# Blocks of 448 query tokens in place of 512 in an attention and two-expert-layer kernel

## The chip, the cores and the metric

The kernel runs on one core of a Trainium2 chip. The metric is the device time of one execution in microseconds (us). PE is the tensor engine, DVE the vector engine, ACT the scalar engine, POOL the GpSimd engine, and SP the engine that issues most transfers. Per-instruction durations are in nanoseconds (ns).

## The reference

The inputs are `q`, `k`, `v` of 12480 tokens by 128 values, 49 agents of 128 values, and four weight matrices between 128 and 2048 values in double precision. The reference computes

```python
scale = 1.0 / np.sqrt(128)
a2k = softmax(scale * agents @ k.T)      # 49 x 12480
agent_v = a2k @ v                        # 49 x 128
q2a = softmax(scale * q @ agents.T)      # 12480 x 49
x = q2a @ agent_v                        # 12480 x 128
h = np.maximum(x @ w_in, 0)
x = (s * h * h + b) @ w_out              # first expert layer
h = np.maximum(x @ w_in2, 0)
out = (h * h) @ w_out2                   # second expert layer
```

## The kernel before

**Precision.** Each large operand is split into two 32-bit words with short mantissas, `hi` and `lo`, whose sum is the operand (`split`, lines 115 to 118). A product then takes two matrix multiplications (`up1`, where the softmaxed scores `X` hold both words in the rows of one operand) or three (`up2` and both `down` products): `lo*hi`, `hi*lo` and `hi*hi`, accumulated in one PSUM bank.

**Stages.** Before the expert layers the kernel goes over keys and values in groups of 1024 tokens (`kblocks`, not part of the change), decodes the double precision weights on DVE between other work (`w_decode`, `fill`), and makes `M`, the agents' values times `w_in` (`m_piece`). So the first layer's up product goes straight from the agent softmax `X` to the hidden values.

**Blocks and steps.** The 12480 queries are cut into blocks by `cut`. A block is `(first token, partitions p, tokens of each partition j)` and holds `n = p * j` tokens; `n` is also the number of columns that every matrix multiplication of its expert layers streams. `cut(4)` gives 24 blocks of 512 (128 partitions of four) and a rest of 192. Because the rest is under 256, the code shares it out with the block before: the list ends with 23 blocks of 512, one of 384 and one of 320, 25 in all. The hidden width of 2048 is 16 chunks of 128, and a step handles two chunks, so that a block has 8 steps (`NPR`). The loop of lines 590 to 634 runs over steps of all blocks in one sequence, and in each step issues, in this order:

- `up1` (line 534): 4 matrix multiplications of the current step, and small pieces of the next block's agent softmax: transposes of its queries (line 133), scores (line 169 with the transposes of line 184, or line 159 for the first four blocks), the exponential, and the stacking transposes of line 215;
- `up2` (line 545): 6 matrix multiplications of the step that is 11 earlier (`L2`);
- `down` of the first layer (line 556): 6 of the step 2 earlier (`LAG`);
- `down` of the second layer (line 556 too): 6 of the step 13 earlier;
- once in 8 steps `store` (line 583): 4 transposes of a finished block's output, a copy, and its transfer.

That is 22 matrix multiplications in a full step, 176 for a block, each with its own weight load. After each `up`, `hidden` runs Relu (line 521) and Square (line 522) on ACT over both chunks at once (1024 elements a partition for a block of 512), then the two parts of `split` on DVE (lines 117 and 118). In steps 1 to 9 the second part runs on POOL instead. Decoding of weights (lines 258 to 278) goes on in DVE's time until about step 19, by a list of operations a step (`FILL_L`).

The order on each engine is written by hand: the program order above is the order of each queue. `ps_h` has two buffers, `ps_y` one for each layer, `ps_m` two.

Of the kernel before, what the change touches and what calls it, by code (L numbers as in the profile page):

```python
# [14 lines left out]
AX = mybir.AxisListType  # L15

P = 128
LAST = 320  # tokens of the last block where the rest is short
LAG = 2  # steps between the two products of a layer
WC = 512  # columns of a weight matrix decoded at a time  # L20
RAW = 4  # weight pieces, groups of keys and groups of values on chip ahead of their use
KB = 5
VB = 7
FIRST = "kwkkwkwkw"  # order of the first loads: keys, weights
# Weight decoding on the vector engine: operations between the others, by phase.
FILL_K = (2, 4, 5, 5, 5, 5, 4, 4, 4, 4, 4, 4, 2, 0)
FILL_T = 1
FILL_V = (5,) * 5 + (3,) * 6 + (1, 0)
QS = (0, 1, 2, 3, 4, 6)  # steps of a block in which the next one's agent softmax is worked on
DIRECT = 4  # blocks before this one have their scores by token at once, with more work on the tensor engine  # L30
M_AT = (2, 3)  # steps before which the last columns of M are made
FM = (2, 2)
FILL_L = (2,) * 6 + (3,) * 5 + (2,) * 2 + (3,) * 10
W_MIN = 2.0**-15
# [4 lines left out]
def tile_agent_attention_two_moe(  # L39
# [15 lines left out]
    _, N, C = q.shape  # L55
# [5 lines left out]
    GAP = 64  # L61
    KS = GAP + NA

    def cut(rows):
        """Token pieces (first token, partitions, tokens of each partition)."""
        pieces, t = [], 0
        while N - t >= rows * P:
            pieces.append((t, P, rows))
            t += rows * P
        if t < N:  # L70
            left = N - t
            p = next(x for x in range(min(P, left), 0, -1) if left % x == 0 and left // x <= rows)
            pieces.append((t, p, left // p))
        return pieces

    blocks = cut(4)
    if len(blocks) > 1 and blocks[-1][1] * blocks[-1][2] < 256:
        # Products this short wait for their weights: the last two blocks share their tokens.
        left = N - blocks[-2][0]
        if left % 4 == 0 and (left - LAST) // 4 <= P:  # L80
            blocks[-2:] = [(blocks[-2][0], (left - LAST) // 4, 4), (N - LAST, LAST // 4, 4)]
    kblocks = cut(8)
    NT = sum(j for _, _, j in kblocks)

# [4 lines left out]
    q, k, v, agents = q[0], k[0], v[0], agents[0]  # L89
# [23 lines left out]
    Xs = [const.tile([KS, 2, 256], F32R, name=f"X{i}") for i in range(2)]  # L113

    def split(dst, src, eng_lo, copy=nc.vector.tensor_copy):
        """dst[0] + dst[1] == src, each with a short mantissa."""
        copy(dst[0], src)  # L117
        eng_lo.tensor_tensor(out=dst[1], in0=src, in1=dst[0].bitcast(F32), op=ALU.subtract)  # L118

# [1 line left out]
    q_raw, qT, q_sT, q_e, q_st, X = {}, {}, {}, {}, {}, {}  # L121

    def q_load(t):
# [26 lines left out]
        q_e[t] = e  # L150

    def q_scores(t):
        """Scores by token, less their maximum."""
        _, p, j = blocks[t]
        x = qT.pop(t)
        ps = ps_m.tile([P, 512], F32, tag="m", name="ps_s")
        sc = ps[:p, :j * NA].rearrange("p (j n) -> p j n", n=NA)
        for i in range(j):
            nc.tensor.matmul(out=sc[:, i], lhsT=x[:, i * p:(i + 1) * p], rhs=aT[:, :NA], start=True, stop=True)
        q_shift(t, sc)  # L160

    def q_scores_T(t):
        """Scores by agent: the agents' short mantissas above, the rest below. The block's halves then go above each other."""
        _, p, j = blocks[t]
        n = p * j
        x = qT.pop(t)
        ps = ps_m.tile([P, 512], F32, tag="m", name="ps_sT")
        for z in (1, 0):
            nc.tensor.matmul(out=ps[:KS, :n], lhsT=aS, rhs=x[z][:, :n], start=(z == 1), stop=(z == 0))  # L169
        sT = sTs[t % 2]  # L170
        for h, to in halves:
            nc.scalar.copy(sT[to, :2 * p], ps[:NA, 2 * p * h:2 * p * (h + 1)])
        for h, to in halves:
            nc.vector.tensor_tensor(
                out=sT[to, :2 * p], in0=ps[GAP:KS, 2 * p * h:2 * p * (h + 1)], in1=sT[to, :2 * p], op=ALU.add
            )
        q_sT[t] = sT
# [29 lines left out]
        q_st[t] = st  # L207

    def q_stack(t):
        """The block's halves come out above each other: each keeps its short mantissas there, the rest goes to the other's rows."""  # L210
        _, p, j = blocks[t]
        st = q_st.pop(t)
        ps = ps_m.tile([P, 512], F32, tag="m", name="ps_x")
        for i in range(2):
            nc.tensor.transpose(  # L215
                out=ps[:KS, i * p:(i + 1) * p],
                in_=st[:p, 2 * i:2 * i + 2].rearrange("p h n -> p (h n)")[:, :KS],
                identity=ident[:p, :p],
            )
        x = Xs[t % 2]  # L220
        places = (0, slice(0, NA), slice(GAP, KS)), (1, slice(GAP, KS), slice(0, NA))
        for h, own, _ in places:
            nc.scalar.copy(x[own, h, :2 * p], ps[own, :2 * p])
        for h, own, other in places:
            nc.vector.tensor_tensor(
                out=x[other, h, :2 * p], in0=ps[own, :2 * p], in1=x[own, h, :2 * p].bitcast(F32), op=ALU.subtract
            )
        X[t] = x[:, :, :2 * p]
# [2 lines left out]
    dec_p = ctx.enter_context(tc.tile_pool(name="dec_p", bufs=3))  # L231

    def w_load(src, i):
        """512 columns of a double precision matrix, as words."""
        t = raw_p.tile([P, WC, 2], I32, tag="raw", name="raw")
        words = src.bitcast(I32)
        if src.shape[0] == P:
            nc.sync.dma_start(
                out=t, in_=words[:, 2 * WC * i:2 * WC * (i + 1)].rearrange("p (f w) -> p f w", w=2)
            )  # L240
        else:
            m = WC // C
            nc.sync.dma_start(
                out=t.rearrange("p (m c) w -> p m (c w)", c=C),
                in_=words[m * P * i:m * P * (i + 1), :].rearrange("(m p) c -> p m c", p=P),
            )
        return t

    def w_decode(raw, hi, lo, early):
        """Double to hi (12 bits of significand) + lo (the 24 bits behind them, rounded)."""  # L250
        L, H = raw[:, :, 0], raw[:, :, 1]
        x = dec_p.tile([P, WC], I32, tag="x", name="x")
        li = dec_p.tile([P, WC], I32, tag="li", name="li")
# [27 lines left out]
    wo_f = [x.rearrange("p m c -> p (m c)") for x in wo]  # L281
    wo2_f = [x.rearrange("p m c -> p (m c)") for x in wo2]

    # Weights are decoded in the vector engine's spare time, two pieces by turns.
    to_load, loaded, running, done = [], [], [], []
    wi = wo2_f  # free until the second layer's last weights come
    for src, pair in ((w_in, wi), (w_out, wo_f), (w_in2, wi2), (w_out2, wo2_f)):
        for i in range(NW):
            to_load.append((src, i, pair))
# [4 lines left out]
            loaded.append((w_load(src, i), i, pair))  # L294

    def fill(n):
        """The next n operations of the decoding; a freed buffer is loaded again."""
        for _ in range(n):
            if len(running) < 2 and loaded and (not running or min(x[1] for x in running) >= 4):
                raw, i, pair = loaded.pop(0)  # L300
# [16 lines left out]
                next_load()  # L317

    def finish(n):
        """Until no more than n pieces are left to decode."""  # L320
        while len(to_load) + len(loaded) + len(running) > n:
            fill(1)

    def m_piece(i):
        """512 columns of the values of the agents times w_in, the same in both halves of the rows."""
        sl = slice(i * WC, (i + 1) * WC)
        ps = ps_m.tile([P, 512], F32, tag="m", name="ps_M")
        for z, (x, w) in enumerate(((av[0], wi[1]), (av[1], wi[0]), (av[0], wi[0]))):
            nc.tensor.matmul(out=ps[:KS], lhsT=x, rhs=w[:, sl], start=(z == 0), stop=(z == 2))
        split((M[0][:, sl], M[1][:, sl]), ps[:KS], nc.vector, nc.scalar.copy)  # L330

    with tc.manual_schedule():
# [1 line left out]
        with tc.tile_pool(name="pre", bufs=1) as pre, tc.tile_pool(name="kp", bufs=2) as kp:  # L334
            NG = len(kblocks)
            ag = pre.tile([NA, C], F32, name="ag")
# [36 lines left out]
                else:  # L373
                    next_load()

            # The tensor engine's clock rises while the first loads are under way.
            ps = ps_m.tile([P, 512], F32, tag="m", name="ps_w")
            for i in range(16):
                nc.tensor.transpose(out=ps[:, :P], in_=ident, identity=ident)
# [65 lines left out]
            ps_cs = ps_y.tile([P, 512], F32, tag="y2", name="ps_cs")  # L445

            def colsum(a, e):
                """Column sums of w_out on every partition: the constant in the first activation adds b times them."""
                for n in range(a, e):
                    w = wo_f[n % 2][:, n // 2 * WC:(n // 2 + 1) * WC]  # L450
                    nc.tensor.matmul(out=ps_cs, lhsT=ones_r, rhs=w, start=(n == 0), stop=(n == 2 * NW - 1))
# [58 lines left out]
                m_piece(i)  # L510
                fill(FM[i])

# [1 line left out]
        ep = ctx.enter_context(tc.tile_pool(name="ep", bufs=2))  # L514
        gp = ctx.enter_context(tc.tile_pool(name="gp", bufs=3))
        L2 = NPR + LAG + 1
# [11 lines left out]
        def up1(t, i):  # L528
            n = blocks[t][1] * blocks[t][2]
            ps = ps_h.tile([P, 2, 512], F32, tag="h", name="ps_h1")  # L530
            for c in range(2):
                sl = slice((2 * i + c) * P, (2 * i + c + 1) * P)
                for z in (1, 0):
                    nc.tensor.matmul(out=ps[:, c, :n], lhsT=M[z][:, sl], rhs=X[t], start=(z == 1), stop=(z == 0))  # L534
            # The vector engine still decodes weights while the first steps run.
            G1[t, i] = hidden(ps, n, 1, nc.gpsimd if 1 <= t * NPR + i < L2 - 1 else nc.vector)

        def up2(t, i):
# [51 lines left out]
        for st in range(total + L2 + LAG + 3):  # L590
            t, i = divmod(st, NPR)
# [73 lines left out]
```

## Time and profile before

| | us |
|---|---|
| three timed runs | 1154.88, 1157.58, 1157.71 |
| median of the runs | 1157.58 |
| profiled execution: span from the first to the last instruction | 1152.7 |
| median less that span | 4.9 |
| PE busy in the span | 1130.1 |
| DVE busy in the span | 961.9 |
| ACT busy in the span | 923.2 |

The profiled execution's own time is not recorded apart from its span; the 4.9 us between span and median are start and end of an execution. "Busy" is the union of an engine's instructions; matrix multiplications are pipelined and overlap, so that the mean duration of one is longer than the distance between two starts. That distance is called the pitch below.

### The profile page before, as it was taken

The numbers are of one execution on the slowest core, as the hardware profiler recorded it, in microseconds if no ns is written. First come the engines' busy times: TensorE is split into PE (matmuls) and PEld (weight loads), VectorE is DVE, ScalarE is ACT, GpSimd is POOL, SyncE is SP. The second block draws the span as 40 slices with busy tenths as digits, with TensorE's granted clock in tenths as the row PEclk, the third lists the DMA queues.
The fourth block names the chain that finished last, engine by engine and source line by source line (L and its number), as shares of the span: only waits on it lengthen the run. The fifth ranks groups of instructions, "written<-read, shape, count | busy, mean of one in ns | idle before, by whom it ended". The sixth has DMA issues, their size and how long they took to land.

```text
span 1152.7 us, 14084 instructions
## 1 busy us (share of the span) xinstructions
PE 1130.1 (98%) x5297; PEld 927.3 (80%) x5297; DVE 961.9 (83%) x1293; ACT 923.2 (80%) x1067; POOL 38.1 (3%) x45
## 2 busy tenths in 40 slices
PE   8997899999999999999999999999999999999998
PEld 8975688888888888888888888888888888888897
DVE  5889998888888888888888888888888888888875
ACT  4646788888888888888888888888888888888885
POOL 1315100000000000000000000000000000000000
PEclk9899999999999999999999999999999999999999
DMA  8860000000000000000000000000000000000000
GB/s 316 243 192 34 1 1 19 19 1 19 19 1 19 19 1 19 19 1 19 19 1 19 19 1 19 19 1 19 19 1 19 19 1 17 15 1 10 10 11 13
DMA packets 27356, 34.88 MB, mean 30 GB/s; under 512 B 1767, under 2 KB 18488, under 8 KB 27288
## 3 DMA queue, kind: packets, MB, share of 16 engines
q1 hardware_dynamic: 27000, 33.98, 9.2%
q8 instruction: 42, 0.69, 0.3%
q14 instruction: 26, 0.21, 0.1%
q10 hardware_dynamic: 288, 0.00, 0.0%
HBM read 27.58 MB, written 6.39 MB: 29 GB/s over the span
## 4 chain that ended last, share of the span: by engine, by line
PE 88%; DVE 5%; ACT 1%; issue 1%; POOL 0%; DVEq 0%; ACTq 0%
PE ps_y L556 46%; PE ps_h L545 24%; PE ps_h L534 15%; PE ps_o L583 1%; PE ps_sT L169 1%; PE ps_q L133 1%; DVE gh L117 1%; ACT r L521 1%; DVE x L264 0%; PE ps_x L215 0%; POOL gl L118 0%; DVE x L270 0%; ACT r L522 0%; DVE li L266 0%; PE ps_b L184 0%
## 5 line engine op out<-in xcount | busy, mean ns | idle before, releaser
L521 ACT ACTIVATE r<-ps_h 128x1024 f32<-128x1024 f32 (+2 forms) x400 | 400.1, 1000 | 145.8 <-PE ps_h L534 121.6
L118 DVE TENSOR_TENSOR gl<-r,gh 128x1024 fp32r<-128x1024 f32 (+2 forms) x391 | 468.5, 1198 | 13.4
L522 ACT ACTIVATE r<-r 128x1024 f32<-128x1024 f32 (+2 forms) x400 | 416.1, 1040 | 12.7
L117 DVE CAST gh<-r 128x1024 fp32r<-128x1024 f32 (+2 forms) x400 | 273.1, 683 | 144.0 <-ACT r L522 139.0
L545 PE MATMUL ps_h<-yh,wi2l 128*128 128x512 f32 (+2 forms) x400 | 162.0, 405 | 2.0 <-DVE yh L117 1.7
L556 PE MATMUL ps_y<-gl,woh 128*128 128x512 f32 (+2 forms) x400 | 156.7, 392 | 5.6 <-POOL gl L118 5.0
L534 PE MATMUL ps_h<-X,Ml 113*128 113x512 f32 (+2 forms) x400 | 158.5, 397 | 1.6 <-DVE Ml L118 0.8
L556 PE MATMUL ps_y<-gh,wol 128*128 128x512 f32 (+2 forms) x400 | 157.7, 394 | 0.5 <-ACT y L564 0.5
L556 PE MATMUL ps_y<-gl,wo2h 128*128 128x512 f32 (+2 forms) x400 | 157.1, 393 | 0.6 <-DVE gl L118 0.6
L534 PE MATMUL ps_h<-X,Mh 113*128 113x512 f32 (+2 forms) x400 | 156.7, 392 | 0.0
L556 PE MATMUL ps_y<-gh,wo2l 128*128 128x512 f32 (+2 forms) x400 | 156.6, 392 | 0.0
L545 PE MATMUL ps_h<-yl,wi2h 128*128 128x512 f32 (+2 forms) x400 | 156.4, 391 | 0.2 <-DVE yl L118 0.2
L545 PE MATMUL ps_h<-yh,wi2h 128*128 128x512 f32 (+2 forms) x400 | 156.5, 391 | 0.0
L556 PE MATMUL ps_y<-gh,wo2h 128*128 128x512 f32 (+2 forms) x400 | 156.2, 391 | 0.0
L556 PE MATMUL ps_y<-gh,woh 128*128 128x512 f32 (+2 forms) x400 | 156.0, 390 | 0.0
L556 PEld LDWEIGHTS ps_y<-gl,woh 128*128 128x128 f32 x400 | 75.4, 189 | 25.4 <-POOL gl L118 7.1
L534 PEld LDWEIGHTS ps_h<-X,Ml 113*128 113x128 f32 x400 | 75.9, 190 | 19.1 <-issue 1.2
L556 PEld LDWEIGHTS ps_y<-gh,woh 128*128 128x128 f32 x400 | 76.0, 190 | 17.3
L556 PEld LDWEIGHTS ps_y<-gh,wol 128*128 128x128 f32 x400 | 75.4, 188 | 17.8 <-ACT y L564 0.9
L534 PEld LDWEIGHTS ps_h<-X,Mh 113*128 113x128 f32 x400 | 75.9, 190 | 16.8
L556 PEld LDWEIGHTS ps_y<-gl,wo2h 128*128 128x128 f32 x400 | 75.2, 188 | 17.1 <-DVE gl L118 1.1
L556 PEld LDWEIGHTS ps_y<-gh,wo2h 128*128 128x128 f32 x400 | 75.2, 188 | 17.1
(122 smaller groups left out, 989.5 us busy)
## 6 DMA issues: line engine op xcount, KB each, us to landing
kraw<-in_k_dram SPq DMA_DIRECT2D x12, 512.0 KB, 7.6
v<-in_v_dram SPq DMA_DIRECT2D x12, 512.0 KB, 7.6
q_raw<-in_q_dram SPq DMA_DIRECT2D x23, 256.0 KB, 2.7
out_dram<-o SPq DMA_DIRECT2D x23, 256.0 KB, 2.0
raw<-in_moe_w_in_dram SPq DMA_DIRECT2D x8, 512.0 KB, 7.2
raw<-in_moe_w_out_dram SPq DMA_DIRECT2D x8, 512.0 KB, 5.1
q_raw<-in_q_dram SPq DMA_DIRECT2D x1, 192.0 KB, 2.6
out_dram<-o SPq DMA_DIRECT2D x1, 192.0 KB, 2.1
```

The source lines that it names most:

```text
L117: copy(dst[0], src)
L118: eng_lo.tensor_tensor(out=dst[1], in0=src, in1=dst[0].bitcast(F32), op=ALU.subtract)
L133: nc.tensor.transpose(out=ps[:, i * p:(i + 1) * p], in_=raw[:p, i], identity=ident[:p, :p])
L169: nc.tensor.matmul(out=ps[:KS, :n], lhsT=aS, rhs=x[z][:, :n], start=(z == 1), stop=(z == 0))
L521: nc.scalar.activation(r[:, :, :n], ps[:, :, :n], AF.Relu)
L522: nc.scalar.activation(r[:, :, :n], r[:, :, :n], AF.Square)
L534: nc.tensor.matmul(out=ps[:, c, :n], lhsT=M[z][:, sl], rhs=X[t], start=(z == 1), stop=(z == 0))
L545: nc.tensor.matmul(out=ps[:, c, :n], lhsT=w[:, sl], rhs=y[:, :n], start=(z == 0), stop=(z == 2))
L556: nc.tensor.matmul(out=py[t][:, :n], lhsT=wz[:, m], rhs=g[:, c, :n], start=(m == 0 and z == 0), stop=(m == NCH - 1 and z == 2),)
L583: nc.tensor.transpose(out=po[:, i], in_=x[:, i * p:(i + 1) * p], identity=ident)
```

## The change

Query blocks are cut at 112 partitions of four tokens, 448 in place of 512. `cut` gets a second argument `most`, the largest number of partitions, which the keys' `cut(8)` leaves at 128. 12480 tokens make 27 blocks of 448 and one of 384 (96 partitions of four): 28 blocks in the place of 25. The code that shared the last tokens between two short blocks goes, as it isn't needed. Nothing else of the program changes; the diff also takes comments and docstrings out, which shifts line numbers.

```diff
-LAST = 320  # tokens of the last block where the rest is short
+BP = 112
...
-    def cut(rows):
+    def cut(rows, most=P):
...
         pieces, t = [], 0
-        while N - t >= rows * P:
-            pieces.append((t, P, rows))
-            t += rows * P
+        while N - t >= rows * most:
+            pieces.append((t, most, rows))
+            t += rows * most
         if t < N:
             left = N - t
-            p = next(x for x in range(min(P, left), 0, -1) if left % x == 0 and left // x <= rows)
+            p = next(x for x in range(min(most, left), 0, -1) if left % x == 0 and left // x <= rows)
             pieces.append((t, p, left // p))
         return pieces
 
-    blocks = cut(4)
-    if len(blocks) > 1 and blocks[-1][1] * blocks[-1][2] < 256:
-        # Products this short wait for their weights: the last two blocks share their tokens.
-        left = N - blocks[-2][0]
-        if left % 4 == 0 and (left - LAST) // 4 <= P:
-            blocks[-2:] = [(blocks[-2][0], (left - LAST) // 4, 4), (N - LAST, LAST // 4, 4)]
+    blocks = cut(4, BP)
     kblocks = cut(8)
```

## Rows read from the trace of the kernel before

**Rows 1.** The page's first lines: busy time, share of the span, instructions.

```profile
span 1152.7 us, 14084 instructions
...
PE 1130.1 (98%) x5297; PEld 927.3 (80%) x5297; DVE 961.9 (83%) x1293; ACT 923.2 (80%) x1067; POOL 38.1 (3%) x45
```

**Rows 2.** Busy time by stretch; columns stand in the second line.

```profile
core 0: us, PE busy (x) PEld busy (x) DVE busy (x) ACT busy (x) POOL busy (x), PEclk, DMA share, GB/s
0.00:81.47 81.47, 73.39 (x544) 69.35 (x544) 60.98 (x124) 40.92 (x71) 16.16 (x36) 0.96 0.83 264
81.47:159.52 78.05, 68.30 (x283) 51.27 (x284) 76.31 (x106) 59.46 (x68) 21.97 (x9) 0.96 0.04 14
159.52:191.12 31.60, 31.60 (x140) 25.46 (x139) 27.05 (x36) 26.72 (x30) 0.00 (x0) 1.00 0.06 18
191.12:1089.22 898.10, 898.10 (x3992) 726.41 (x3991) 753.18 (x967) 751.71 (x841) 0.00 (x0) 1.00 0.04 12
1089.22:1152.69 63.47, 58.72 (x345) 54.78 (x343) 44.39 (x63) 44.41 (x60) 0.00 (x0) 0.98 0.03 11
```

**Rows 3.** Waits from 191.12 to 1089.22 us: total, times, longest.

```profile
DVE gh L117 <- ACT r L522: 121.6, 151, 1.2
ACT r L521 <- PE ps_h L534: 110.5, 126, 1.4
ACT e L192 <- DVE e L149: 20.7, 21, 1.0
```

**Rows 4.** Busy time by stretch: three steps of one block of 512, its sum.

```profile
620.98:626.56 5.58, 5.58 (x28) 4.53 (x27) 4.24 (x6) 4.49 (x6) 0.00 (x0) 1.00 0.00 0
...
637.53:642.69 5.16, 5.16 (x24) 4.14 (x23) 4.44 (x7) 4.25 (x5) 0.00 (x0) 1.00 0.00 0
...
647.85:653.36 5.51, 5.51 (x28) 4.45 (x26) 5.02 (x10) 4.71 (x6) 0.00 (x0) 1.00 0.01 3
...
sum 42.99, PE 42.99 PEld 34.65 DVE 36.06 ACT 35.98 POOL 0.00; mean PE 5.37 PEld 4.33 DVE 4.51 ACT 4.50 POOL 0.00
```

**Rows 5.** The same view: one step, 384 columns in layer one, 512 in layer two.

```profile
1065.83:1070.38 4.55, 4.55 (x24) 4.01 (x23) 3.74 (x6) 4.00 (x5) 0.00 (x0) 1.00 0.00 0
```

**Rows 6.** PE's timeline: two starts 12 instructions apart, 320 columns each.

```profile
1137.66 0.31 PE L545 MATMUL ps_h<-yh,wi2l 128*128 128x320 f32 x1
...
1139.42 0.31 PE L545 MATMUL ps_h<-yh,wi2l 128*128 128x320 f32 x1
```

**Rows 7.** Groups by line and shape: busy us, mean ns, idle before, releasers.

```profile
L118 DVE TENSOR_TENSOR gl<-r,gh 128x1024 fp32r<-128x1024 f32 x359 | 439.9, 1225 | 12.3
L522 ACT ACTIVATE r<-r 128x1024 f32<-128x1024 f32 x368 | 390.8, 1062 | 11.7
L521 ACT ACTIVATE r<-ps_h 128x1024 f32<-128x1024 f32 x368 | 375.9, 1021 | 129.8 <-PE ps_h L534 112.7 <-POOL gl L118 9.9 <-DVE gl L118 4.4
L117 DVE CAST gh<-r 128x1024 fp32r<-128x1024 f32 x368 | 256.3, 696 | 130.1 <-ACT r L522 125.3 <-issue 0.2
...
L556 PEld LDWEIGHTS ps_y<-gh,woh 128*128 128x128 f32 x400 | 76.0, 190 | 17.3
...
L118 POOL TENSOR_TENSOR gl<-r,gh 128x1024 fp32r<-128x1024 f32 x9 | 22.0, 2441 | 39.2 <-PE ps_y L556 27.0 <-DVE gh L117 12.2
...
L118 DVE TENSOR_TENSOR gl<-r,gh 128x768 fp32r<-128x768 f32 x16 | 15.3, 959 | 0.6
...
L522 ACT ACTIVATE r<-r 128x768 f32<-128x768 f32 x16 | 13.6, 847 | 0.5
...
L262 DVE TENSOR_SCALAR li<-raw 128x512 int32<-128x512 int32 x16 | 11.8, 739 | 2.3 <-DMA raw<-in_moe_w_in_dram 2.3
...
L521 ACT ACTIVATE r<-ps_h 128x768 f32<-128x768 f32 x16 | 12.9, 808 | 7.8 <-PE ps_h L534 4.6 <-PE ps_h L545 3.0
...
L117 DVE CAST gh<-r 128x768 fp32r<-128x768 f32 x16 | 9.0, 560 | 7.1 <-ACT r L522 7.1
```

**Rows 8.** DVE's timeline from 115.5 us: one instruction, with start and us.

```profile
116.46 2.58 DVE L262 TENSOR_SCALAR li<-raw 128x512 int32<-128x512 int32 x1
```

## The prediction

> **What bounds the kernel now.** I read the page first: PE is busy for 1130.1 of 1152.7 us, DVE and ACT for 83% and 80% [rows 1]. A share over the whole span says little about a stage, so I cut the span into stretches [rows 2]. Three things are to be seen there. From 159.52 us until the last block enters at 1089.22 us, PE is busy for every microsecond, at a granted clock of 1.00, which is the 2.4 GHz level. Between 81.47 and 159.52 us (the first 18 steps) it is DVE that is busy for 76.31 of 78.05 us, PE for 68.30. Before 81.47 us no expert layer runs, and after 1089.22 us the pipeline drains. Then I read the waits of the full stretch: DVE waits for ACT and ACT for PE, and PE waits for nobody [rows 3]. So 898 us of the span are the sum of the pitches of PE's instructions, and what the change does there is a question about one number: the pitch of a matrix multiplication of 448 columns.
>
> **What the pitch is at the three lengths that the trace has.** A plain step of a 512 block is 22 matrix multiplications in 5.16 us [rows 4], so 234.55 ns each. In the step of rows 5 layer one streams 384 columns (10 instructions) and layer two 512 (12): 4.55 us less 12 x 234.55 ns leaves 1.735 us, so 173.5 ns for 384 columns [rows 5]. In the drain 12 instructions of 320 columns take 1139.42 less 1137.66 us, so 146.7 ns [rows 6]. At the 2.4 GHz that the trace shows as granted, one column a cycle would be 213.3, 160.0 and 133.3 ns. The excess is thus 21.2 ns at 512, 13.5 at 384 and 13.4 at 320. Weight loads do not set it: each is listed at 190 ns [rows 7], yet the 320-column instructions follow each other at 146.7 ns, so the loads run beside them.
>
> No row shows 448. The nearest rows bound it from both sides. If the excess stays at 13.5 ns, 448 columns take 186.7 + 13.5 = 200.2 ns; if it is already at 21.2, 207.9 ns. The straight line between the rows of 384 and 512 gives 204.0. A smooth curve through all three rows, which bends because the excess doesn't grow from 320 to 384, gives 202.8. I take 203.4, half way between line and curve, and keep 200.2 and 207.9 as ends.
>
> **The change, part by part.** The columns streamed in all stay the same; 28 blocks issue 4928 matrix multiplications where 25 issued 4400.
>
> *The full stretch.* 176 x 203.4 ns is 35.80 us a block. To this come the small pieces that a block has on PE whatever its size. Before, they are 42.99 less 8 x 5.16, so 1.71 us; the first step of a block (query transposes) has 0.42 of it and the step of the store 0.35 [rows 4]. The store's transposes move 128 columns however many partitions the block has, so its 0.35 stays; the other 1.36 lies between unchanged and 7/8 of itself, which gives 1.54 to 1.71. I take 1.60. A block is then 37.40 us, and the 24 blocks that take the place of the 22 in the 898.10 us [rows 2] take 897.6 us.
>
> *Do ACT and DVE keep up?* Of the four large operations of `hidden`, 896 elements lie half way between the rows of 1024 and 768 [rows 7]. L118 falls by 0.133 us, L117 by 0.068, L521 by 0.107, L522 by 0.108, 16 times a block. DVE goes from 36.06 to 32.9 us a block and ACT from 35.98 to 32.5 [rows 4, 7], 88% and 87% of 37.40, where both were at 84%. PE stays the slowest. The waits of the two engines for PE, 232 us in all [rows 3], are the cover; only with that gone would PE wait.
>
> *The first 18 steps.* DVE sets their time. 25 casts save 0.068 us each (1.7 us), 16 subtractions on DVE 0.133 each (2.1), and small work 0.3. The nine POOL operations of 2441 ns [rows 7] matter too, since a DVE instruction that meets one is held: the same L262 that means 739 ns took 2.58 us [rows 7, 8]. An eighth off each is 0.3 us, 2.75 in all. I take the sum, 6.75 us, so 71.3 in the place of 78.05 us. The bounds are 4.1 (POOL's part gives nothing) and 9.8 (all work shrinks by an eighth; the decoding of weights, unchanged in size, speaks against it). PE's own work there, 240 matrix multiplications, shrinks by 31 ns each or 7.5 us, so it fits.
>
> *Steps 18 to 23.* They take 31.60 us now [rows 2]; 132 x 203.4 ns and 0.64 us of transposes make 27.49.
>
> *The end.* The drain after the last block enters holds 48 instructions of 512, 108 of 384 and 176 of 320 columns: 11.26 + 18.74 + 25.82, with two stores (0.70) 56.5 of the 63.47 us [rows 2]. The other 6.95 us are the last chain through ACT and DVE and the last transfer. After the change it holds 156 of 448 and 176 of 384 columns, 31.73 + 30.54 + 0.70, and the last chain works on 768 elements in the place of 640, half of the step between the two rows of each operation: 0.133 + 0.068 + 0.107 + 0.108 = 0.42 us more, 7.37. Total 70.3 us, 6.9 more, because the last block is larger and the blocks in flight are others.
>
> *At nothing.* The start to 81.47 us is keys, values and weights, which keep their cut; three more query loads and three more stores run on SP's queue, with DMA at 4% of the full stretch [rows 2].
>
> **The sum**, against the profiled span: 81.47 + 71.3 + 27.49 + 897.6 + 70.3 = 1148.2 us, 4.5 less than 1152.7. The median of the runs stands 4.9 us above that span, and I let it keep its distance: 1157.58 - 4.5 = 1153.1 us, 0.4% faster. One nanosecond of pitch is worth 4512 instructions x 1 ns, 4.5 us: the unknown price decides everything. A difference of 0.3% (3.5 us) is about what a measurement of this kernel can tell from none.
>
> **Rule against row.** The row says that 512 columns take 234.55 ns and 384 take 173.5 [rows 4, 5], so the excess is no constant. The Trainium skill ("TensorE: Matmul & The Clock Gate", section "Back-to-back issue gap") gives the isolated gap as columns at 2.4 GHz and a fixed 2.5 ns for each instruction; no run here shows that figure, and the trace's excess is five to eight times as large. By it the 528 added instructions would cost 528 x 2.5 ns, 1.3 us, and nothing would be gained on columns, where my pitches make all matrix multiplications together 8.7 us shorter (1005.8 to 997.1); the result would be 10.0 us above mine, about 1163 us. It is a smaller size of the first rival below and has a quarter of that rival's chance, since the trace's excess doesn't have its form.
>
> **The rivals.**
>
> *Each instruction has a fixed price.* The place is PE's pitch in all 4512 instructions outside the first steps, the price the excess of 21.2 ns that 512 shows: 207.9 ns, 4.5 ns above mine, 20.3 us more, 1173.4. From 204.6 ns on the change is slower than the median before. The constant excess from 320 to 384 speaks for a fixed price; that it is 13.5 there and not 21.2 [rows 5, 6] speaks against this size. Chance 0.2.
>
> *Only the full 512 columns pay extra.* The excess rises by 7.7 ns somewhere between 384 and 512; if 448 lies before that rise it pays 13.5: 200.2 ns, 14.4 us less, 1138.6. The flat piece from 320 to 384 speaks for it; nothing shows where the rise is. Chance 0.2.
>
> *The change doesn't shorten the first steps.* If decoding and POOL's hold on DVE keep the 18 steps at 78.05 us, though they carry an eighth fewer tokens, the 6.75 us come back: 1159.9. DVE's 98% there [rows 2] speaks for it, the shorter operations against. Chance 0.05.
>
> *ACT or DVE becomes the bound in the full stretch.* At 88% they would need 12% more work; bunched in the second step of a block this could make PE wait some 0.2 us a block, 5 us, 1158. Chance 0.05.
>
> **How the numbers follow.** My forecast has 0.5, with a range of its own from line and curve, one nanosecond to each side of 203.4: 1149 to 1158. The range that holds 8 in 10 goes half way into the two large rivals: 1143 to 1166. Faster by over 0.3% (under 1154.1): the second rival whole and half of my case, 0.46. Slower by over 0.3% (over 1161.1): the first rival whole and a part of the small ones and of my case's edge, 0.25. Between: 0.29.
>
> **What the profile after would show.** Right: a plain step of 22 instructions in about 4.47 us and a block in 37.40, PE busy for the whole of the full stretch, no wait of PE there, ACT and DVE busy for about 32.5 us a block, the first 18 steps in about 71 us. Wrong: a plain step under 4.42 (second rival) or over 4.55 us (first), PE rows in the waits of the full stretch, or first steps that last as long as before. The prediction is wrong above all if the pitch isn't smooth in the number of columns.

## The result and the profile after

The kernel with blocks of 448 takes 1147.18 us (median of 4 runs, 1145.01 to 1147.49), the kernel before 1156.23 us (4 runs, 1154.55 to 1157.71). The ratio is 0.9918, with a 95% interval from 0.9898 to 0.9937: 0.8% faster. The forecast was 1153.1 us, 0.4% faster than the median then shown, in a range from 1143 to 1166. The runs of each kernel fall in two groups 2 to 3 us apart (before 1154.55 and 1154.88, then 1157.58 and 1157.71; after 1145.01, then 1147.11 to 1147.49), so that the gain is 9.05 us between the medians and 9.7 to 10.4 us from group to group.

The first lines of the page of the kernel after answer to [rows 1]; the third is the granted TensorE clock in 40 slices.

```profile
span 1145.1 us, 15590 instructions
...
PE 1117.9 (98%) x5867; PEld 1031.9 (90%) x5867; DVE 983.8 (86%) x1431; ACT 941.3 (82%) x1187; POOL 38.3 (3%) x45
...
PEclk7899999999999999999999999999999999999999
```

PE has 570 instructions more and is busy for 12.2 us less. The span is 7.6 us shorter than the span before. Busy time by stretch, cut at the same places of the program as [rows 2], shows where (columns as there: PE, PEld, DVE, ACT, POOL, granted clock, DMA share, GB/s):

```profile
0.00:84.13 84.13, 74.37 (x544) 70.52 (x544) 61.02 (x124) 40.76 (x71) 17.43 (x36) 0.88 0.81 255
84.13:154.56 70.43, 58.05 (x283) 48.74 (x284) 69.17 (x105) 53.03 (x67) 20.83 (x9) 1.00 0.05 15
154.56:181.83 27.27, 27.27 (x140) 25.39 (x139) 25.04 (x36) 24.64 (x30) 0.00 (x0) 1.00 0.06 19
181.83:1075.26 893.43, 893.43 (x4562) 826.60 (x4561) 779.83 (x1105) 773.71 (x961) 0.00 (x0) 1.00 0.04 13
1075.26:1145.07 69.81, 64.79 (x345) 60.64 (x343) 48.79 (x64) 49.13 (x60) 0.00 (x0) 0.98 0.03 10
```

| stretch | before | forecast | after |
|---|---|---|---|
| start, up to the first step | 81.47 | 81.47 | 84.13 |
| first 18 steps | 78.05 | 71.3 | 70.43 |
| steps 18 to 23 | 31.60 | 27.49 | 27.27 |
| full stretch (22 blocks, then 24) | 898.10 | 897.6 | 893.43 |
| last block and drain | 63.47 | 70.3 | 69.81 |
| span | 1152.69 | 1148.2 | 1145.07 |

In the full stretch PE is again busy for every microsecond. The windows of one of its blocks answer to [rows 4]: the first step, a plain one, the step of the store, and the block as a whole.

```profile
554.17:559.10 4.93, 4.93 (x28) 4.48 (x27) 3.90 (x6) 4.13 (x6) 0.00 (x0) 1.00 0.00 0
568.57:573.01 4.44, 4.44 (x24) 4.13 (x23) 3.73 (x7) 3.24 (x6) 0.00 (x0) 1.00 0.00 0
...
577.45:582.25 4.80, 4.80 (x28) 4.43 (x26) 4.49 (x9) 4.26 (x6) 0.00 (x0) 1.00 0.02 3
554.17:591.40 37.23, 37.23 (x192) 34.44 (x191) 32.49 (x47) 32.23 (x41) 0.00 (x0) 1.00 0.05 13
```

A plain step of 22 matrix multiplications takes 4.44 us: the pitch at 448 columns is 201.8 ns, an excess of 15.1 ns over one column a cycle. The small pieces of a block are 37.23 - 8 x 4.44 = 1.71 us, as before. The waits of the full stretch answer to [rows 3]: DVE waits for ACT and ACT for PE, though less than before, and PE's matrix multiplications wait for nobody; the one row that names PE's side is weight loads, 2.5 us in 893, with no idle time of PE behind it.

```profile
DVE gh L112 <- ACT r L517: 80.9, 144, 0.9
ACT r L516 <- PE ps_h L529: 73.9, 143, 0.9
...
PEld ps_b L179 <- DVE sT L169: 2.5, 16, 0.2
```

Groups by line and shape answer to [rows 7]; after the change, lines are five lower. The four operations of 896 elements came out within 1 ns of the half-way estimate (1092, 629, 915 and 956 ns measured; 1092, 628, 914 and 955 expected). The mean of POOL's nine operations fell by 5% only, but one of them took 3390 ns in this profile; their median went from 2385 to 2114 ns, 11% less and close to the eighth that was forecast.

```profile
L113 DVE TENSOR_TENSOR gl<-r,gh 128x896 fp32r<-128x896 f32 x423 | 462.0, 1092 | 14.5
L517 ACT ACTIVATE r<-r 128x896 f32<-128x896 f32 x432 | 413.0, 956 | 13.7
L516 ACT ACTIVATE r<-ps_h 128x896 f32<-128x896 f32 x432 | 395.3, 915 | 102.1 <-PE ps_h L529 74.7 <-POOL gl L113 10.4 <-DVE gl L113 10.2
L112 DVE CAST gh<-r 128x896 fp32r<-128x896 f32 x432 | 271.6, 629 | 100.1 <-ACT r L517 88.0 <-PE ps_o L578 8.3
...
L113 POOL TENSOR_TENSOR gl<-r,gh 128x896 fp32r<-128x896 f32 x9 | 20.8, 2319 | 35.2 <-DMA raw<-in_moe_w_out_dram 25.1 <-DVE gh L112 10.1
```

### The profile page after: what moved, and what is told of

It reads as the page before. It is cut to its first block, busy times and chain, and to the rows that moved or that the text cites. A ratio compares the mean times of both kernels' runs of the same rounds, so it can differ in the third digit from the quotient of the medians.

```text
span 1145.1 us, 15590 instructions
## 1 busy us (share of the span) xinstructions
PE 1117.9 (98%) x5867; PEld 1031.9 (90%) x5867; DVE 983.8 (86%) x1431; ACT 941.3 (82%) x1187; POOL 38.3 (3%) x45
## 4 chain that ended last, share of the span: by engine, by line
PE 87%; DVE 5%; ACT 1%; issue 1%; POOL 0%; DVEq 0%; ACTq 0%
PE ps_y L551 45%; PE ps_h L540 23%; PE ps_h L529 15%; PE ps_o L578 1%; DVE gh L112 1%; PE ps_sT L164 1%; PE ps_q L128 1%; ACT r L516 0%; DVE gl L113 0%; DVE x L265 0%; DVE li L261 0%; PE ps_x L210 0%; PE ps_b L179 0%; POOL gl L113 0%; DVE x L259 0%
## 5 line engine op out<-in xcount | busy, mean ns | idle before, releaser
L516 ACT ACTIVATE r<-ps_h 128x896 f32<-128x896 f32 (+1 forms) x448 | 408.4, 912 | 110.8 <-PE ps_h L529 77.6
L113 DVE TENSOR_TENSOR gl<-r,gh 128x896 fp32r<-128x896 f32 (+1 forms) x439 | 477.3, 1087 | 15.1
L517 ACT ACTIVATE r<-r 128x896 f32<-128x896 f32 (+1 forms) x448 | 426.6, 952 | 14.2
L112 DVE CAST gh<-r 128x896 fp32r<-128x896 f32 (+1 forms) x448 | 280.5, 626 | 108.8 <-ACT r L517 96.7
L540 PE MATMUL ps_h<-yh,wi2l 128*128 128x448 f32 (+1 forms) x448 | 170.5, 381 | 3.4 <-ACT r L516 1.8
L551 PE MATMUL ps_y<-gl,woh 128*128 128x448 f32 (+1 forms) x448 | 162.9, 364 | 6.3 <-POOL gl L113 5.8
L529 PE MATMUL ps_h<-X,Ml 113*128 113x448 f32 (+1 forms) x448 | 166.5, 372 | 0.8 <-DVE Ml L113 0.8
L529 PE MATMUL ps_h<-X,Mh 113*128 113x448 f32 (+1 forms) x448 | 164.0, 366 | 0.0
L540 PE MATMUL ps_h<-yl,wi2h 128*128 128x448 f32 (+1 forms) x448 | 162.8, 363 | 0.1
L540 PE MATMUL ps_h<-yh,wi2h 128*128 128x448 f32 (+1 forms) x448 | 162.8, 363 | 0.0
L540 PEld LDWEIGHTS ps_h<-yh,wi2l 128*128 128x128 f32 x448 | 84.2, 188 | 10.8 <-ACT r L516 3.1
```

Of the source, the lines that this page charges most:

```text
L516: nc.scalar.activation(r[:, :, :n], ps[:, :, :n], AF.Relu)
L517: nc.scalar.activation(r[:, :, :n], r[:, :, :n], AF.Square)
L540: nc.tensor.matmul(out=ps[:, c, :n], lhsT=w[:, sl], rhs=y[:, :n], start=(z == 0), stop=(z == 2))
L551: nc.tensor.matmul(out=py[t][:, :n], lhsT=wz[:, m], rhs=g[:, c, :n], start=(m == 0 and z == 0), stop=(m == NCH - 1 and z == 2),)
```

## The experiments

The theory after the result: all that the change gains is the pitch, 201.8 ns at 448 in the place of 234.55 at 512, less a price of some 1.7 us for each further block. The first question was what the excess is, the second what sets it.

**PE's stream alone.** Groups of six matrix multiplications, each with its own weights, and nothing else at work beside them (shortened, `...` marks what is left out):

```python
for n in SIZES + ("zero",) + SIZES:
    ...
    for g in range(8):
        ...
        for m in range(6):
            nc.tensor.matmul(out=ps[:, :n], lhsT=w[:, m], rhs=xs[m % 2][:, :n], start=(m == 0), stop=(m == 5))
```

> This kernel leaves the whole computation out: it streams groups of six matrix multiplications with 12 lengths from 512 to 128 columns, twice, each with its own weights as in the expert layers, with ACT, DVE and POOL idle, and once 512 columns of zeros between the two passes. Theory: the excess over one column a cycle belongs to PE's instruction itself and isn't proportional to the columns, so the pitches of the kernel come back: 234 ns at 512, 202 at 448, 174 at 384, 147 at 320. Rival one, contention with ACT and DVE: the excess is smaller here and about the same at all lengths, 512 under 229 ns. Rival two, only the full bank of 512 columns pays: 496 and 480 columns have the 13 to 15 ns of 384 and 448, so 496 takes 220 to 222 ns and only 512 takes 234.

**The same with ACT and DVE busy.** After every second group, Relu, Square, cast and subtraction of 1024 elements on other tiles.

> The same streams with ACT and DVE made busy by the four operations of one step of 1024 elements after every second group, on tiles of their own; the computation is left out here too. Theory: the pitches are those of the quiet streams within 1 ns. Rival, contention: they are longer by several ns at every length, and 512 rises to 234 ns only here.

Pitches in ns, worked out from the starts in the traces (mean over the instructions of a length with data), and the excess over one column at 2.4 GHz:

```
columns      512    496    480    464    448    432    416    384    352    320    256    128
quiet      226.7  220.0  216.6  209.9  202.7  195.7  188.4  173.3  161.0  146.6  119.9  110.6
busy       226.7  220.0  216.6  209.9  202.7  195.6  188.4  173.3  161.0  146.6  119.9  110.6
excess      13.3   13.3   16.6   16.6   16.0   15.7   15.1   13.3   14.3   13.3   13.2   57.3
```

Three things follow. The load of ACT and DVE changes nothing: they were busy for 89.0 and 82.5 of 180 us beside PE. Rival one's sign, 512 under 229 ns, did come in the quiet run, but the busy run doesn't bring 234 ns back (contention falls; the run on all columns below has the higher load). There is a floor: no length has a mean excess under 13.2 ns, and 13.3 ns are 32 cycles at 2.4 GHz; 512, 496, 384, 320 and 256 sit on it. And what lies above the floor is not smooth: 480 has 16.6 and 496 only 13.3. The single starts show why a mean hides this: at 480 the gaps alternate between 213 and 221 ns, at 464 between 205 and 215, while at 496 each is 220. My theory of an excess that belongs to the length alone failed for 512, which took 226.7 ns here and 234.55 in the kernel. The zeros, which follow 128 columns, begin with eight gaps of 225 to 236 ns and then repeat 227, 227, 226 like the data. So a stream of 512 columns can have gaps as long as the kernel's, but here it leaves them after eight instructions. Zeros and data of 512 columns together have a mean of 227.7 ns, the figure in one of the expectations below.

**Other block lengths in the whole kernel.** The kernel after with `BP = 120` (26 equal blocks of 480) and with `BP = 126` (24 blocks of 504 and one of 384).

> 26 equal blocks of 480 tokens. Theory, an excess that grows by degrees from 448 (15 ns) to 512 (21 ns): 18 ns at 480, so a pitch of 218 ns; the matrix multiplications then take 997.6 us where 448 takes 989.5, two blocks fewer give 3.2 us of small pieces back, so about 5 us slower than blocks of 448 and 0.4% faster than 512. Rival, only the full 512 columns pay: 215 ns, 984 us, 9 us faster than blocks of 448 and 1.5% faster than 512.

> 24 blocks of 504 tokens and one of 384, so 25 blocks as before the change: no block more, and the short block of 320 is gone as with 448. Theory, an excess that grows by degrees: 20 ns at 504, a pitch of 230 ns, about 4 us (0.3%) faster than 512. Rival, only the full 512 columns pay: 225 ns, 25 us (2%) faster. Rival, the gain of the change came from the last blocks and not from the length: the same 0.8% as with 448.

Blocks of 480: 1149.71 us, ratio 0.9941 (0.9925 to 0.9957). Blocks of 504: 1144.80 us, ratio 0.9905 (0.9886 to 0.9924). The block windows of the two profiles, 480 first, then 504 and a plain step of 504:

```profile
307.86:347.87 40.01, 40.01 (x192) 34.54 (x191) 34.30 (x47) 34.17 (x41) 0.00 (x0) 1.00 0.05 13
```

```profile
315.28:357.17 41.89, 41.89 (x192) 34.60 (x191) 35.62 (x47) 35.59 (x41) 0.00 (x0) 1.00 0.04 13
331.44:336.46 5.02, 5.02 (x24) 4.14 (x23) 4.30 (x7) 4.01 (x5) 0.00 (x0) 1.00 0.00 0
```

504 needs 5.02 us for a plain step, 228.2 ns; a plain step of 480 takes 4.794 us by its starts, 217.9 ns. Eight columns fewer than 512 (1.6%) make a matrix multiplication 2.7% shorter. 504 has 25 blocks as before, so a gain needs no other number of blocks. Nor do the last blocks carry it: 480 has no short block at all and gains less than 504 and 448, which keep one of 384 (and 416, below, has none and gains nothing). In the profile of 504 it is the full stretch of 22 blocks that shrinks, from 898.10 to 879.52 us, while the last block and drain grow from 63.47 to 73.48. The intervals of 504 and 448 overlap, so that these two can't be told apart.

**What throws 512 off.** First the step's stream exactly as the kernel issues it (four products, shapes, order), without the other engines; then the same with the first layer's up product on 128 rows and one contiguous operand in the place of 113 rows and two halves.

> PE's stream of a step as the kernel issues it, with tiles of the same shapes, at 14 lengths from 512 to 384, eight steps each; all other engines and all dependencies between steps are left out, and so is the computation. Theory: the pitch has a floor of the columns and 32 cycles of 2.4 GHz (13.3 ns), which equal instructions in a row can hold, and the four instructions of the first layer's up product (113 rows, two halves) throw the stream off it; 512 is then long in getting back: about 234 ns here, 201 to 202 at 448, 228 at 504. Rival: the 7 ns that 512 pays in the kernel beyond the 227.7 ns of the quiet stream come from waits and signals between the engines; then 512 takes 227 to 228 ns here too.

> The same stream with the first layer's up product on 128 rows and one contiguous operand; the computation is left out here too. Theory: with nothing to throw the stream off, 512 takes 227 to 228 ns and 448 takes 200 to 201. Rival: it is the change of weights, banks and operands between the four products of a step, whatever their shape: 512 takes 234 ns as in the kernel.

Then the stream of the pattern with the kernel's waits and signals, ACT and DVE working on 8 columns, and on all columns:

```diff
+        k = WORK or n
+        nc.scalar.activation(r[:, :, :k], ps[:, :, :k], AF.Relu)
+        nc.scalar.activation(r[:, :, :k], r[:, :, :k], AF.Square)
+        nc.vector.tensor_copy(gh[:, :, :k], r[:, :, :k])
+        nc.vector.tensor_tensor(out=gl[:, :, :k], in0=r[:, :, :k], in1=gh[:, :, :k].bitcast(F32), op=ALU.subtract)
```

> The step's stream with the kernel's signals and waits between PE, ACT and DVE, but with ACT and DVE working on 8 columns only, so that they load nothing; 12 lengths, eight steps each. The computation is left out. Theory: the waits and signals throw the stream of 512 off its best rhythm: about 234 ns at 512 where the stream without them took 228.5, and 448 near 202 where it took 206. Rival, the load of ACT and DVE on the memories: the pitches are those without signals, 228.5 at 512 and 206 at 448.

> The same with ACT and DVE working on all the block's columns, as in the kernel. Both theories: the kernel's pitches, 234.5 at 512, 228 at 504, 218 at 480, 202 at 448. If both this and the run with 8 columns stay at 228.5 ns for 512, the cause is neither, and something else of the kernel sets the rhythm.

Pitches in ns (a plain step by 22), with those of the whole kernels in the last line:

```
columns                   512    504    500    496    480    448    416    384
pattern                 228.5  227.9  227.0  223.8  217.0  206.1  188.9  173.9
128 rows, contiguous    226.7  226.7  223.3  223.3  216.7  206.7  186.7  173.3
waits, 8 columns        228.5  227.9  227.0  223.8  217.0  206.1  188.9  173.9
waits, all columns      228.5  227.9  227.0  223.8  217.0  206.1  188.9  173.9
whole kernel            234.5  228.2  224.5  224.5  217.9  201.8  189.4  173.5
```

Waits, signals and load change nothing within 0.2 ns, though ACT and DVE were nearly as busy as in the kernel in the second of the two (81% and 76% in the window below; 84% each in the block of [rows 4]). The window from 90 to 130 us of the runs with 8 columns, then with all, shows the same PE beside 5.62 and 30.48 us of DVE:

```profile
90.00:130.00 40.00, 40.00 (x177) 32.95 (x176) 5.62 (x32) 6.40 (x32) 0.00 (x0) 1.00 0.00 1
```

```profile
90.00:130.00 40.00, 40.00 (x177) 32.96 (x176) 30.48 (x33) 32.22 (x33) 0.00 (x0) 1.00 0.00 1
```

The shape of the up product is worth 1.8 ns at 512, 3.7 at 500, 2.2 at 416 and under 1.3 elsewhere. For 504, 496, 480, 416 and 384 the kernel's pitch comes within 1 ns of the pattern's; 512 is 6.0 ns above it, 448 is 4.3 below, 500 is 2.5 below. So waits and load fall, and the theory that the up product throws 512 off explains 1.8 of the 7.8 ns by which the kernel lies over the best stream of 512.

The single gaps show where kernel and pattern part (means over plain steps, ns):

```
                          512 kernel  512 pattern  448 kernel  448 pattern
ten up products                234.3        230.7       204.3        205.4
twelve down products           234.8        226.7       199.8        206.7
```

In the pattern the up products disturb the stream of 512, and it is back on its floor before the first `down` product. In the kernel it never gets there: the twelve `down` products of a step are as slow as the rest. At 448 it is the other way round, and the kernel's `down` products are the ones on the floor of 200.0 ns. So most of the difference lies in products of one shape, 128 rows and contiguous, that the pattern issues in the same order.

**Small pieces left out.** The kernel before, without the softmax pieces of blocks 4 to 11 (their scores are those of an earlier block) and with the stores of blocks 4 to 16 untransposed:

```diff
-                if t + 1 < NB:
+                if t + 1 < NB and not soft(t + 1):
+                    X[t + 1] = Xs[(t + 1) % 2]
+                elif t + 1 < NB:
...
-                store(t)
+                (plain_store if 4 <= t < 17 else store)(t)
```

> The kernel before, blocks of 512, with the small pieces on PE left out of part of the full stretch: the agent softmax of blocks 4 to 11 (their scores are those of an earlier block) and the transposes of the stores of blocks 4 to 16 (their outputs are stored untransposed). So PE issues only the 22 matrix multiplications of each step while blocks 4 to 10 enter and the stores of blocks 4 and later fall due, then softmax pieces alone, then all again. Theory one, the small pieces knock the stream of 512 off its best rhythm: a step without them takes 22 x 228.5 ns, 5.03 us, as in the streams alone, and goes back to 5.16 us where they return. Theory two, the rhythm hangs on where the operands lie or on another fixed property of this kernel: 5.16 us a step all through.

A block with only matrix multiplications takes 41.12 us, so 5.14 us a step and 233.6 ns each; with the softmax pieces back but not the store's transposes it takes 42.55.

```profile
357.44:398.56 41.12, 41.12 (x178) 33.15 (x177) 31.75 (x35) 33.76 (x35) 0.00 (x0) 1.00 0.02 7
564.48:607.03 42.55, 42.55 (x188) 34.27 (x187) 35.47 (x46) 35.97 (x41) 0.00 (x0) 1.00 0.04 13
```

The pieces are not what keeps 512 slow: theory one expected 228.5 ns. The same 22 gaps, between 229 and 238 ns, come back in each of the eight steps of that block, so the slow rhythm is steady and no chance of single waits. The run also gives the price of a block's pieces directly: 42.99 - 41.12 = 1.87 us, 0.16 of it because the plain steps take 5.14 us there and not 5.16.

**Looking for a better length.** 24 blocks of 496 and two of 288; 24 of 500 and one of 480 (`BP = 125`); 30 of 416 (`BP = 104`).

> 24 blocks of 496 tokens and two of 288, 26 in all. Theory: the pitch isn't smooth in the columns; if 496 holds its floor of 220.0 ns as in the quiet stream, the matrix multiplications take 24 x 176 x 220.0 + 2 x 176 x 133.3 ns, 976 us, and with two blocks fewer the kernel is 16 us faster than with blocks of 448, so 2.2% faster than with 512. Rival, an excess that grows by degrees between 448 and 512: 226 ns, 1002 us, about 9 us slower than 448 and no faster than 512.

> 24 blocks of 500 tokens and one of 480, 25 blocks as before. The pitch can't be foretold from the length by a smooth rule: the streams without waits took 223.3 or 227.0 ns at 500. With 223.3 the matrix multiplications take 981 us and the kernel is 25 us (2.1%) faster than with 512, with 227.0 997 us and 9 us (0.8%) faster. A smooth rule between 504 (228.2) and 480 (217.9) gives 226.5, 995 us, 11 us (0.9%) faster.

> 30 equal blocks of 416 tokens. The streams without waits took 186.7 and 188.9 ns at 416, so 986 to 997 us of matrix multiplications; five blocks more than 25 cost 1.71 us each in small pieces, 8.6 us. Theory, two terms (the pitch at this length, and a price per block): 1 to 11 us faster than 512, so no better than 448. Rival, shorter blocks go on gaining at the rate from 512 to 448: 0.4% more than 448, 1.2% faster than 512.

496: 1149.90 us, ratio 0.9957 (0.9943 to 0.9970). The floor of 220.0 ns did not come; a plain step of 4.94 us is 224.5 ns, between the two expectations. 500: 1140.21 us, ratio 0.9871 (0.9846 to 0.9896), the fastest of all and faster than 448. 416: 1154.61 us, ratio 0.9990 (0.9977 to 1.0004), no gain. A plain step of 500 and its block, then the block of 416:

```profile
328.20:333.15 4.95, 4.95 (x24) 4.15 (x23) 4.24 (x7) 3.82 (x5) 0.00 (x0) 1.00 0.00 0
312.28:353.58 41.30, 41.30 (x192) 34.73 (x191) 35.42 (x47) 35.32 (x41) 0.00 (x0) 1.00 0.05 13
```

```profile
279.15:314.05 34.90, 34.90 (x192) 34.31 (x191) 30.73 (x47) 30.37 (x41) 0.00 (x0) 1.00 0.05 13
```

By starts a plain step of 500 takes 4.940 us, so 224.5 ns, and one of 416 takes 4.167 us, 189.4 ns. A ledger of two terms, all matrix multiplications at the measured pitch plus the blocks times what a block takes beyond eight plain steps, gives for the equal or nearly equal cuts:

| tokens | blocks | products, us | pieces, us | ledger, us less than 512 | profile from the first step on, us less | medians, us less (1 - ratio, x 1156) |
|---|---|---|---|---|---|---|
| 512 | 25 | 1005.8 | 42.7 | | | |
| 504 | 25 | 994.4 | 43.3 | 10.8 | 10.5 | 11.0 |
| 500 | 25 | 986.8 | 44.5 | 17.2 | 16.0 | 14.9 |
| 480 | 26 | 997.1 | 43.1 | 8.3 | 7.1 | 6.8 |
| 448 | 28 | 989.5 | 47.9 | 11.1 | 10.3 | 9.5 |
| 416 | 30 | 1000.1 | 46.9 | 1.5 | 0.7 | 1.2 |

The order is the ledger's but for 504 and 448, which it has 0.3 us apart, and each size is within 2.3 us. The last column but one has the profiled spans less the time up to their first step, which differs between executions (see the start, below); by it the ledger holds within 1.3 us and is always a little high. 496 with its two blocks of 288 gained 5 us in the medians where the ledger gives about 10. Counted from the first step it gained 8.9 us, so most of what is missing lies before that step, as far as one profile can tell: it came at 85.03 us there.

## Why the prediction was right, and where its sizes were off

**The bound** was read rightly: PE sets the full stretch before and after, no product waits there, and the pitch decides. DVE and ACT came out at 32.49 and 32.23 us a block (32.9 and 32.5 forecast).

**The pitch** is the term that was mis-sized: 203.4 ns forecast, 201.8 measured. 1.6 ns in 4224 instructions are 6.8 us in the full stretch, and 0.5 in the last block and steps 18 to 23. The value lay between my ends of 200.2 and 207.9; but the reason I gave for a place between them, a smooth curve, does not hold. The streams have 448 at 206.1 ns in one rhythm and the kernel at 201.8 in another, and 496 at 220.0 or 223.8. No curve through 320, 384 and 512 could have told 448; the range was what these rows were worth, and that the value fell inside near the middle was luck in part. The prediction had named a pitch that isn't smooth as its chief sign of being wrong, and that sign came. Nor does the number choose between my forecast and the second rival: 201.8 lies half way between 203.4 and the rival's 200.2, and the kernel's `down` products at 448 are at 199.8. (In the first rival, the bound from which the change is slower works out to 204.4 ns, not 204.6.)

**The small pieces** were forecast at 1.60 us a block and stayed at 1.71, 2.6 us more in the full stretch. I took the transposes of 112 partitions as shorter; the first step's excess even grew, from 0.42 to 0.49 us.

**The first 18 steps** (71.3 forecast, 70.43 measured) and **the end** (70.3, 69.81) came out within 1 us. In the first, the four operations and POOL's shrank about as I took them, and six operations of DVE lasted over 1.5 us there where eight had; which of them run into one of POOL's differs between the two profiles. The granted clock rose as well, from 0.96 to 1.00, but the time didn't follow it: with blocks of 512, 480, 448 and 416 the stretch took 78.05, 74.27, 70.43 and 66.88 us, in nearly even steps, at clocks of 0.96, 0.95, 1.00 and 1.00.

**The start** was costed at nothing, and it took 2.66 us longer. It doesn't look like an effect of the change, as there is no order by length: in the profiles of the other lengths the first step begins at 81.65 (500), 81.85 (416), 81.87 (504), 84.15 (480) and 85.03 us (496). From the first step on the kernel gained 10.3 us (1071.22 to 1060.94), more than twice the 4.5 us that I forecast; the late start hid a quarter of it from the spans.

**From span to median** I kept 4.9 us. The profiled execution after took 1147.11 us for its span of 1145.1, so what lies around a span is 2.0 us, and not the 4.9 that I put down to start and end of an execution. The execution whose trace I read was faster than the median of its runs by some 1.5 us (1152.7 + 2.0 against 1156.23; 2.9 against the 1157.58 then shown). Spans fell by 7.6 us, medians by 9.05. In spans the forecast missed 3.1 us: the pitch gave 7.3 more than forecast and the first 18 steps 0.9, the pieces took 2.6 back and the start 2.7, and the last 0.2 is rounding.

**The rivals.** A fixed price per instruction exists: the floor of 13.3 ns. But the 21.2 ns that the first rival needed did not show at 448 (15.1). The rule of the Trainium skill ("TensorE: Matmul & The Clock Gate", section "Back-to-back issue gap") of a fixed 2.5 ns in the isolated gap fits no run here: none had less than 13.2. The part of it that speaks against shorter blocks, a fixed price of each added instruction, is there, five times as large. The second rival, that only the full 512 columns pay, falls in the kernel with 504 (18.2 ns of excess) and 480 (17.9). The two small rivals did not occur.

**What stays open** is why 512 runs at 234.5 ns and 448 at 201.8 in the kernel, when the same stream elsewhere gives 228.5 and 206.1. Each tried by itself, waits, load, the small pieces and (but for 1.8 ns) the up product's shape are excluded; zeros in the place of data were tried in the quiet stream alone. What is left sits mostly in the `down` products, whose shapes and order are the same in both. That the places of the operands in the memories choose the rhythm is a guess that was not tried.

## What to carry to other kernels

Where PE is busy without a gap, cost a change of tile length by the pitch at exactly that length, measured in the kernel, and by the price of one more block; here curves through other lengths missed it by up to 1% (203.4 for 201.8 at 448, 226.5 for 224.5 at 500) and the same stream alone by up to 3%, and one per cent of the pitch is about the whole effect. Try lengths a few columns below the largest: 500 gained 1.3% with no block more, where 448 gained 0.8% with three more; 504, with none more either, can't be told from 448. Subtract spans from spans and medians from medians, since one profiled execution can lie anywhere among the runs.

## What the runs showed of the hardware

The mean pitch of these two-word products has a floor of the columns plus 32 cycles at 2.4 GHz (13.2 to 13.3 ns over one column a cycle, from 256 to 512 columns) with new weights in each, and repeating patterns above it: at 480 columns 213 and 221 ns by turns, at 464 205 and 215. The rhythm isn't fixed by the length and the order of products: in the pattern and in the kernel 512 columns ran at 228.5 and 234.5 ns, 448 columns at 206.1 and 201.8, each time in gaps that repeat. At 128 columns the pitch is 110.6 ns and no longer follows the columns (53.3 ns); what bounds it there, the weight loads perhaps, was not tested.

The start of the kernel differs between executions, and the granted clock differs with it. In the profile with blocks of 500 the windows up to 20 and 45 us show 1.00 in both; after the change studied here 0.72 and 0.95, which is some time at the lower of the two levels of 1.2 and 2.4 GHz, and the first step began 2.5 us later (84.13 against 81.65 us):

```profile
0.00:20.00 20.00, 16.00 (x84) 15.12 (x85) 8.94 (x16) 6.42 (x9) 3.49 (x24) 1.00 0.82 311
20.00:45.00 25.00, 24.81 (x229) 24.68 (x228) 20.98 (x46) 18.63 (x30) 0.00 (x0) 1.00 0.96 280
```

```profile
0.00:20.00 20.00, 15.00 (x73) 14.28 (x74) 8.50 (x15) 5.93 (x7) 3.49 (x24) 0.72 0.83 309
20.00:45.00 25.00, 25.00 (x222) 25.00 (x221) 20.11 (x43) 17.49 (x27) 0.00 (x0) 0.95 1.00 287
```

A slow first window alone does not cost it: the profiles of 504 and 416 had 0.74 there and 1.00 in the second, and began at 81.9 us. The profile of 480 had 0.72 and 0.95 like the one shown, and began at 84.15. That of 496 had 1.00 and 0.99, but 0.81 from 45 to 80 us, where the others have 0.90, and began last, at 85.03. No run held the clock fixed, so that it is the cause is argued, not shown.
